# Transposed attention blocks written to DRAM in two copies and read by one transfer, and the split of v by a sign

## The chip, the cores and the metric

The kernel runs on one core of a Trainium2 chip. The metric is the time of one execution on the device in microseconds (us), the median of the runs shown. The engines of the core are TensorE (PE, with its weight loads PEld), VectorE (DVE), ScalarE (ACT), GpSimd (POOL) and SyncE (SP), which issues all DMAs of this kernel on one queue.

## What is computed

Attention within chunks of 64 tokens, then a layer with the elementwise maximum of three products. The reference, cut:

```python
# q, k, v: (batch 8, heads 8, seq 576, head_dim 64), chunk = 64, scale = 1/sqrt(64)
scores = scale * np.matmul(q_c, k_c.transpose(0, 1, 2, 4, 3))
scores = scores - np.max(scores, axis=-1, keepdims=True)
attn = np.exp(scores)
attn = attn / (np.sum(attn, axis=-1, keepdims=True) + 1e-09)
out = np.matmul(attn, v_c)
...
# x: (4608 tokens, 512), w1, w2, w3: (512, 768), w_out: (768, 512)
h = np.maximum(np.maximum(x @ w1, x @ w2), x @ w3)
return (h @ w_out).astype(np.float32)
```

All in float32.

## The kernel before

**Number format.** PE multiplies operands that are rounded to a narrower form (fp32r). To keep the accuracy, an operand is split into a high part (a rounding copy on ACT) and a low part (operand minus high part), and `three` adds three matmuls: high by low, low by high, high by high. One such trio of 128x512 is called a block here. Where both operands carry their parts, the products of the attention use another form: one operand is stacked, high part in partitions 0 to 63 and low part in 64 to 127, and the other holds high and low side by side in the free direction; a matmul then gives two sums that are added on the way out of PSUM (`products`: ACT copies one, VectorE adds the other).

**Tiles.** The tokens are 36 tiles of 128 (two chunks each, eight heads), in nine groups of four. The first eight tiles go through `plain_steps` at the start of the kernel, written in an order by hand (`FIRST`). The other 28 go through `attention`, whose steps are spread among the matmuls of the layer of earlier groups (`moe`; the last two groups are done together in `pair`). The tail after the last tile does no attention.

**One tile in `attention`.** r (q and k, two loads of 512 KB) is split into qs (stacked) and kk (side by side). Two products s, one for each chunk of the tile (steps s0 and s1), are summed into e by `sa0` and `sa1`. Then: maximum (`mx`, VectorE), subtraction (`sub`, POOL), exponential (`exp`, ACT), sum, guard and reciprocal (`sum`, VectorE), normalization (`nrm`, POOL), transpose of 32x32 blocks (`T`, VectorE) into et, high part (`ah`, ACT) and low part (`al`, VectorE) of et into the tile ah. The transposed blocks have to change partitions, so SP writes ah to a DRAM tile called there (`there`), waits, and reads it back as aa (`aa`), twice, into partitions 0 to 63 and 64 to 127, since v is stacked with its high part in the one half and its low part in the other. v (rv, 512 KB, each value in both halves) becomes vs: rounding copy of all 128 partitions on ACT (`vh`), and rv minus that copy in partitions 64 to 127 on POOL (`vl`, in `stack`, L311). Two products x of vs and aa (steps x0 and x1, in one bank of PSUM after another use of it) are summed into xs, or into the tile stage for the last two groups; where there is no stage, xs is split into xh (`xh`, ACT) and xl (`xl`, VectorE) for the layer. The tiles rv, kk, qs, r, ah and aa have one buffer each.

**What sets the order.** Inside `tc.manual_schedule` the instructions of each engine stand in the order in which the code emits them, and each engine works in that order. `due` collects a tile's steps with a time each: the table `AT` for the first four of these tiles, `MOVED` on top of it for the other 24. The main loop counts 0.6815 us for a block and 0.49 us for four products, and emits each step when its time has come. So the numbers of the tables only place a step between blocks; on the chip it starts when its semaphores allow. `TIMES` puts the tiles 18.0 us apart at first and 14.9 us from the fifth on. `FIRST_MIXED` places the first combinations of weights for `pair`.

Of the kernel before, what the change touches and what calls it, by code (L numbers as in the profile page):

```python
# [9 lines left out]
F32 = mybir.dt.float32  # L10
F32R = mybir.dt.float32r
# [3 lines left out]
AF = mybir.ActivationFunctionType  # L15
ALU = mybir.AluOpType
AX = mybir.AxisListType
# [3 lines left out]
P = 128  # L21
# [11 lines left out]
MOVED = {'r0': -18.9, 'r1': -14.6, 'rv': 7.3, 'qh': -8.4, 'ql': -7.2, 'kh0': -7.1, 'kl0': -6.2, 'kh1': -5.6, 'kl1': -1.4, 'sa0': 1.3, 's1': 3.3, 'sa1': 4.3, 'mx': 4.6, 'sub': 5.9, 'exp': 6.9, 'sum': 7.9, 'nrm': 9.1, 'T': 10.5, 'ah': 11.6, 'al': 11.7, 'there': 13.9, 'aa': 16.3, 'vh': 16.8, 'vl': 18.3, 'x0': 24.6, 'xa0': 25.6, 'x1': 28.3, 'xa1': 29.6, 'xh': 30.6, 'xl': 31.4}  # L33
EVERY = [18.3, 15.6]
OPERANDS = 5.4
FIRST_MIXED = 5.6
# [35 lines left out]
def chunk_attn_maxout_kernel(  # L72
# [12 lines left out]
    nc = tc.nc  # L85
# [21 lines left out]
    make_identity(nc, ident)  # L107

# [160 lines left out]
    def attention(t, x_of, col, every, stage=None, moved=()):  # L269
# [11 lines left out]
        def due(at, pe=0.0):  # L281
            return lambda fn: ops.append((at, pe, fn))
# [103 lines left out]
        @due(at_["al"])  # L386
        def _():
            nc.vector.tensor_tensor(out=st["ah"][:, :, 1], in0=st["et"], in1=st["ah"][:, :, 0].bitcast(F32), op=ALU.subtract)

        @due(at_["there"])  # L390
        def _():
            st["there"] = dram.tile([4, 64, 512], F32, name="there")
            nc.sync.dma_start(out=st["there"].rearrange("n (l k) f -> (n l) k f", k=2),
                              in_=st["ah"].bitcast(F32).rearrange("p k a n x -> p k (a n x)"))

        @due(at_["aa"])
        def _():
            st["aa"] = att.tile([P, 4, 2, 8, 32], F32R, name="aa", tag="aa", bufs=1)
            for rows in halves_of:
                nc.sync.dma_start(out=st["aa"][rows].bitcast(F32).rearrange("p n a g x -> p n (a g x)"),  # L400
                                  in_=st["there"].rearrange("n p f -> p n f"))

        stack(at_["vh"], at_["vl"], "vs", f"vs{t % 2}", lambda: st["rv"], nc.gpsimd)
# [17 lines left out]
        @due(at_["xl"])  # L421
        def _():
            xh, xl = x_of()
            nc.vector.tensor_tensor(out=xl[:, :, col:col + P], in0=st["xs"], in1=xh[:, :, col:col + P].bitcast(F32),
                                    op=ALU.subtract)
# [496 lines left out]
```

## Time and profile before

| | |
|---|---|
| median of 3 runs | 714.03 us (713.11 to 722.75) |
| profiled execution | 720.41 us, of which its span is 718.6 us |
| mean granted clock of PE | 0.983 |
| bytes moved by DMA | 125.93 MB, mean 175 GB/s |
| the queue of SP | busy 57.8% of 16 engines' span |

In the rows of the waits stand the engine and line that waited, what it waited for, the total in us, the number of waits and the longest. In the chain stand start, duration and what ran. In the groups of instructions stand line, engine, operation, output and inputs, shapes, count, busy time in us, mean duration in ns, and behind the second bar the idle time before them with what ended it; rows with three durations split by slashes give the least, the median and the greatest in ns. In the rows of DMA issues stand count, size of each and median us from issue to landing. In the rows of windows stand the window, its length, busy time and count of PE, PEld, DVE, ACT and POOL, the granted clock, the busy share of the DMA engines and GB/s. An arrow "x<-aa,vs" names output and inputs by the tiles' names. L289 is the matmul of the attention products, L169 to L171 the three of a block, L300 the sum on the way out of PSUM.

### The profile page before, as it was taken

The numbers are of one execution on the slowest core, as the hardware profiler recorded it, in microseconds if no ns is written. First come the engines' busy times: TensorE is split into PE (matmuls) and PEld (weight loads), VectorE is DVE, ScalarE is ACT, GpSimd is POOL, SyncE is SP. The second block draws the span as 40 slices with busy tenths as digits, with TensorE's granted clock in tenths as the row PEclk, the third lists the DMA queues.
The fourth block names the chain that finished last, engine by engine and source line by source line (L and its number), as shares of the span: only waits on it lengthen the run. The fifth ranks groups of instructions, "written<-read, shape, count | busy, mean of one in ns | idle before, by whom it ended". The sixth has DMA issues, their size and how long they took to land.

```text
span 718.6 us, 9620 instructions
## 1 busy us (share of the span) xinstructions
PE 691.3 (96%) x3336; PEld 574.5 (80%) x3336; DVE 516.7 (72%) x868; ACT 376.5 (52%) x695; POOL 249.9 (35%) x182
## 2 busy tenths in 40 slices
PE   8999999998899999999999998999989999999997
PEld 5998888887778777878877777878778888888876
DVE  6699984777668876898577876788657486768630
ACT  4476754554655566566656654566555352334221
POOL 1232201333334344222432332223323438666510
PEclk9599999999999999999999999999999999999999
DMA  8765554565787879667887767677784401011011
GB/s 344 304 226 180 205 176 138 173 207 172 224 258 215 220 209 277 177 202 213 236 232 194 214 175 236 195 212 193 194 257 123 131 30 59 29 31 26 5 55 63
DMA packets 44944, 125.93 MB, mean 175 GB/s; under 512 B 4192, under 2 KB 4192, under 8 KB 44896
## 3 DMA queue, kind: packets, MB, share of 16 engines
q1 hardware_dynamic: 44896, 125.32, 57.8%
q8 instruction: 26, 0.43, 0.3%
q14 instruction: 22, 0.18, 0.1%
HBM read 98.83 MB, written 26.48 MB: 174 GB/s over the span
## 4 chain that ended last, share of the span: by engine, by line
PE 29%; DMA 15%; DVE 13%; POOL 8%; ACT 4%; issue 3%; SPq 1%; POOLq 0%; ACTq 0%; DVEq 0%
DMA aa<-there 11%; PE pm L169 8%; PE pm L171 8%; PE pm L170 8%; DMA there<-ah 4%; PE x L289 3%; POOL c L537 2%; PE s L289 2%; POOL e L667 2%; DVE c L543 2%; POOL m L670 1%; DVE e L300 1%; POOL e L186 1%; POOL f L523 1%; ACT e L295 1%
## 5 line engine op out<-in xcount | busy, mean ns | idle before, releaser
L169 PE MATMUL pm<-xh,wl 128*128 128x512 f32 (+1 forms) x516 | 201.7, 391 | 0.0
L171 PE MATMUL pm<-xh,wh 128*128 128x512 f32 (+1 forms) x516 | 200.5, 389 | 0.0
L170 PE MATMUL pm<-xl,wh 128*128 128x512 f32 (+1 forms) x516 | 200.2, 388 | 0.0
L311 POOL TENSOR_TENSOR vs<-rv,vs 64x1024 fp32r<-64x1024 f32 x28 | 67.2, 2401 | 205.9 <-ACT vs L307 160.4
L171 PEld LDWEIGHTS pm<-xh,wh 128*128 128x128 f32 x516 | 98.0, 190 | 20.6
L169 PEld LDWEIGHTS pm<-xh,wl 128*128 128x128 f32 x516 | 98.3, 191 | 16.6
L170 PEld LDWEIGHTS pm<-xl,wh 128*128 128x128 f32 x516 | 98.1, 190 | 16.6
L300 DVE TENSOR_TENSOR e<-s,e 64x256 f32<-64x256 f32 x112 | 47.2, 422 | 47.6 <-ACT e L295 46.4
L458 DVE TENSOR_TENSOR m<-pm,m 128x512 f32<-128x512 f32 (+1 forms) x86 | 58.2, 677 | 11.9 <-PE pm L171 9.7
L169 PE MATMUL pm<-woh,h 128*128 128x512 f32 x168 | 65.6, 391 | 0.0
L170 PE MATMUL pm<-wol,h 128*128 128x512 f32 x168 | 65.6, 390 | 0.0
L171 PE MATMUL pm<-woh,h 128*128 128x512 f32 x168 | 65.5, 390 | 0.0
L186 POOL TENSOR_TENSOR e<-e,sm 128x512 f32<-128x512 f32 x30 | 37.6, 1253 | 73.4 <-DVE sm L183 58.4
L289 PEld LDWEIGHTS x<-aa,vs 128*128 128x128 f32 x224 | 32.4, 188 | 32.0 <-issue 17.5
L289 PE MATMUL x<-aa,vs 128*128 128x256 f32 x224 | 37.8, 291 | 20.0 <-DMA aa<-there 16.2
L295 ACT COPY e<-s 64x256 f32<-64x256 f32 x112 | 41.1, 367 | 28.5 <-PE s L289 27.5
L359 POOL TENSOR_TENSOR e<-e,mx 128x512 f32<-128x512 f32 x28 | 36.9, 1318 | 37.3 <-DVE mx L355 37.3
L464 ACT CAST h<-m 128x512 fp32r<-128x512 f32 (+1 forms) x43 | 26.2, 609 | 41.6 <-DVE m L458 41.4
L295 ACT COPY xs<-x 64x256 f32<-64x256 f32 x80 | 29.4, 368 | 33.2 <-PE x L289 32.5
L300 DVE TENSOR_TENSOR xs<-x,xs 64x256 f32<-64x256 f32 x80 | 33.4, 417 | 12.4 <-ACT xs L295 10.5
L337 DVE TENSOR_TENSOR kk<-r,kk 128x512 fp32r<-128x512 f32 x56 | 41.3, 739 | 1.0 <-ACT kk L333 0.8
L311 DVE TENSOR_TENSOR qs<-r,qs 64x1024 fp32r<-64x1024 f32 x28 | 37.5, 1340 | 6.1 <-ACT qs L307 5.4
(121 smaller groups left out, 1293.6 us busy)
## 6 DMA issues: line engine op xcount, KB each, us to landing
r<-in_qk SPq DMA_DIRECT2D x56, 512.0 KB, 4.6
aa<-there SPq DMA_DIRECT2D x56, 512.0 KB, 6.8
rv<-in_v SPq DMA_DIRECT2D x28, 512.0 KB, 5.5
there<-ah SPq DMA_DIRECT2D x28, 512.0 KB, 2.8
out_x<-ao SPq DMA_DIRECT2D x36, 256.0 KB, 2.1
buf<-in_qk SPq DMA_DIRECT2D x8, 768.0 KB, 7.2
buf<-in_w SPq DMA_DIRECT2D x10, 512.0 KB, 3.4
buf<-in_vb SPq DMA_DIRECT2D x8, 512.0 KB, 4.3
```

The lines of the kernel that those rows point to most:

```text
L169: nc.tensor.matmul(out=o, lhsT=al, rhs=bh, start=first, stop=False)
L170: nc.tensor.matmul(out=o, lhsT=ah, rhs=bl, start=False, stop=False)
L171: nc.tensor.matmul(out=o, lhsT=ah, rhs=bh, start=False, stop=last)
L186: eng.tensor_tensor(out=e, in0=e, in1=sm.unsqueeze(2).broadcast_to([P, 8, 64]), op=ALU.mult)
L289: nc.tensor.matmul(out=o[:, g].rearrange("p a h x -> p (a h x)"), lhsT=lhs(g), rhs=rhs(g), start=True, stop=True)
L295: nc.scalar.copy(out=out()[rows], in_=st[name][rows, :, 0, h, :])
L300: nc.vector.tensor_tensor(out=out()[rows], in0=st[name][rows, :, 1, h, :], in1=out()[rows], op=ALU.add)
L311: eng.tensor_tensor(out=st[name][64:], in0=src()[64:], in1=st[name][64:].bitcast(F32), op=ALU.subtract)
L337: nc.vector.tensor_tensor(out=st["kk"][:, c, :, 1, :], in0=st["r"][:, 1, c], in1=st["kk"][:, c, :, 0, :].bitcast(F32), op=ALU.subtract)
L359: nc.gpsimd.tensor_tensor(out=e_all(), in0=e_all(), in1=st["mx"].unsqueeze(2).broadcast_to([P, 8, 64]), op=ALU.subtract)
L458: nc.vector.tensor_tensor(out=banks[j][:, :n], in0=ps[j, w][:, :n], in1=banks[j][:, :n], op=ALU.max)
L464: nc.scalar.copy(out=hh[j][:, lo:hi], in_=banks[j][:, :hi - lo])
```

## The change

For each of the 28 tiles of `attention`:

- The write of ah goes out in two copies by one DMA: there is 1 MB instead of 512 KB, and each pair of its rows appears twice, next to itself.
- One DMA reads it into all 128 partitions; before, two read the same 512 KB into 64 partitions each. High and low parts of v therefore no longer lie in the two halves: partition 4l + 2h + k holds the high part for h = 0 and the low part for h = 1, and the host lays out v in that order.
- Since an instruction works on a range of partitions and the parts now alternate in pairs, vs is made in all partitions at once: ACT makes rv times a sign (+1 for high, -1 for low, from the new tile `sign_of`), rounded; VectorE then adds rv times 0 or 1 (`is_low`), over 128x1024 elements. `is_low` and `sign_of` are made by two operations on VectorE at the start.
- The subtractions `al` (28 times) and `xl` (20 times) go from VectorE to POOL, and `vl` from POOL to VectorE.
- Most numbers of `MOVED` change by 0.1 to 3.3 us and `FIRST_MIXED` by 0.2.

```diff
-MOVED = {... 'al': 11.7, 'there': 13.9, 'aa': 16.3, 'vh': 16.8, 'vl': 18.3, 'x0': 24.6, 'xa0': 25.6, 'x1': 28.3, ...}
+MOVED = {... 'al': 13.7, 'there': 13.9, 'aa': 17.5, 'vh': 17.4, 'vl': 18.6, 'x0': 25.1, 'xa0': 26.1, 'x1': 28.6, ...}
-FIRST_MIXED = 5.6
+FIRST_MIXED = 5.4
...
+    is_low, sign_of = (cpool.tile([P, 1], F32, name=n) for n in ("is_low", "sign_of"))
+    nc.vector.tensor_reduce(out=is_low, in_=ident.rearrange("p (l h k) -> p l h k", h=2, k=2)[:, :, 1], axis=AX.XY, op=ALU.add)
+    nc.vector.tensor_scalar(out=sign_of, in0=is_low, scalar1=-2.0, scalar2=1.0, op0=ALU.mult, op1=ALU.add)
...
         @due(at_["al"])
         def _():
-            nc.vector.tensor_tensor(out=st["ah"][:, :, 1], in0=st["et"], in1=st["ah"][:, :, 0].bitcast(F32), op=ALU.subtract)
+            nc.gpsimd.tensor_tensor(out=st["ah"][:, :, 1], in0=st["et"], in1=st["ah"][:, :, 0].bitcast(F32), op=ALU.subtract)
...
-            st["there"] = dram.tile([4, 64, 512], F32, name="there")
-            nc.sync.dma_start(out=st["there"].rearrange("n (l k) f -> (n l) k f", k=2),
-                              in_=st["ah"].bitcast(F32).rearrange("p k a n x -> p k (a n x)"))
+            st["there"] = dram.tile([4, P, 512], F32, name="there")
+            nc.sync.dma_start(out=st["there"].rearrange("n (l h k) f -> (n l) h (k f)", h=2, k=2),
+                              in_=st["ah"].bitcast(F32).rearrange("p k a n x -> p (k a n x)").unsqueeze(1)
+                              .broadcast_to([P, 2, 1024]))
...
-            for rows in halves_of:
-                nc.sync.dma_start(out=st["aa"][rows].bitcast(F32).rearrange("p n a g x -> p n (a g x)"),
-                                  in_=st["there"].rearrange("n p f -> p n f"))
-
-        stack(at_["vh"], at_["vl"], "vs", f"vs{t % 2}", lambda: st["rv"], nc.gpsimd)
+            nc.sync.dma_start(out=st["aa"].bitcast(F32).rearrange("p n a g x -> p n (a g x)"),
+                              in_=st["there"].rearrange("n p f -> p n f"))
...
+            nc.scalar.activation(out=st["vs"], in_=st["rv"], func=AF.Copy, scale=sign_of)
...
+            nc.vector.scalar_tensor_tensor(out=st["vs"], in0=st["rv"], scalar=is_low, in1=st["vs"].bitcast(F32),
+                                           op0=ALU.mult, op1=ALU.add)
...
-            nc.vector.tensor_tensor(out=xl[:, :, col:col + P], in0=st["xs"], in1=xh[:, :, col:col + P].bitcast(F32),
+            nc.gpsimd.tensor_tensor(out=xl[:, :, col:col + P], in0=st["xs"], in1=xh[:, :, col:col + P].bitcast(F32),
```

What the table makes of the order shows at three places, all in the steady part, at the seventeenth of the 28 tiles. On SP's queue, before, from the write of one tile to its second load of r:

```order
L393 DMA there<-ah 128x1024
L320 DMA r<-in_qk 128x1024
L400 DMA aa<-there 64x4x512 x2
L325 DMA rv<-in_v 128x1024
L320 DMA r<-in_qk 128x1024
```

And in the changed kernel:

```order
L396 DMA there<-ah 256x1x1024
L323 DMA r<-in_qk 128x1024
L403 DMA aa<-there 128x4x512
L328 DMA rv<-in_v 128x1024
L323 DMA r<-in_qk 128x1024
```

The sequence is the same; the write has twice the rows, and one read stands for two. Next, VectorE from the transpose of one tile (et) to the maximum of the next (mx), before:

```order
L379 STREAM_TRANSPOSE et<-e 128x512
L300 TENSOR_TENSOR xs<-x,xs 64x4x64 x2
L388 TENSOR_TENSOR ah<-et,ah 128x2x256
L337 TENSOR_TENSOR kk<-r,kk 128x4x128
L458 TENSOR_TENSOR m<-pm,m 128x512
L300 TENSOR_TENSOR xs<-x,xs 64x4x64 x2
L300 TENSOR_TENSOR e<-s,e 64x4x64 x2
L424 TENSOR_TENSOR xl<-xs,xh 128x4x128
L458 TENSOR_TENSOR m<-pm,m 128x512
L300 TENSOR_TENSOR e<-s,e 64x4x64 x2
L467 TENSOR_TENSOR h<-m,h 128x512
L355 TENSOR_REDUCE mx<-e 128x8
```

The same stretch in the changed kernel, where the names are the same and the lines have moved:

```order
L382 STREAM_TRANSPOSE et<-e 128x512
L303 TENSOR_TENSOR xs<-x,xs 64x4x64 x2
L340 TENSOR_TENSOR kk<-r,kk 128x4x128
L469 TENSOR_TENSOR m<-pm,m 128x512
L303 TENSOR_TENSOR xs<-x,xs 64x4x64 x2
L340 TENSOR_TENSOR kk<-r,kk 128x4x128
L303 TENSOR_TENSOR e<-s,e 64x4x64 x2
L469 TENSOR_TENSOR m<-pm,m 128x512
L413 SCALAR_TENSOR_TENSOR vs<-rv,is_low,vs 128x1024
L478 TENSOR_TENSOR h<-m,h 128x512
L303 TENSOR_TENSOR e<-s,e 64x4x64 x2
L358 TENSOR_REDUCE mx<-e 128x8
```

The low parts of ah and xl are gone, the second low part of kk has come into this stretch, and the low part of vs stands, with a low part of h, ahead of the sum of the second score product and the maximum. Last, POOL over one tile, before:

```order
L186 TENSOR_TENSOR e<-e,sm 128x512
L311 TENSOR_TENSOR vs<-rv,vs 64x1024
L359 TENSOR_TENSOR e<-e,mx 128x512
L186 TENSOR_TENSOR e<-e,sm 128x512
L311 TENSOR_TENSOR vs<-rv,vs 64x1024
```

And in the changed kernel:

```order
L189 TENSOR_TENSOR e<-e,sm 128x512
L391 TENSOR_TENSOR ah<-et,ah 128x2x256
L435 TENSOR_TENSOR xl<-xs,xh 128x4x128
L362 TENSOR_TENSOR e<-e,mx 128x512
L189 TENSOR_TENSOR e<-e,sm 128x512
```

Between the normalization of one tile and the subtraction of the next now stand the low part of ah and that of an earlier tile's xl, instead of the low part of vs.

On PE no instruction is added or removed. Counted in its order, 28 blocks stand between the second score product (s1) and the first product x (x0) of a tile before, and 29 in the changed kernel, for 24 of the 28 tiles (the first four keep 27 or 28); between x0 and x1 there are 5 blocks before and 4 in the changed kernel. x1 keeps its place.

9 lines of the change are left out of this document (7 added, 2 removed).

## The prediction

> **What bounds the kernel now.** I read the busy shares first, then what TensorE (PE) waits for, then the chain that ended last, then the transfers.
>
> ```profile
> span 718.6 us, 9620 instructions
> PE 691.3 (96%) x3336; PEld 574.5 (80%) x3336; DVE 516.7 (72%) x868; ACT 376.5 (52%) x695; POOL 249.9 (35%) x182
> ```
>
> PE is idle in only 718.6 - 691.3 = 27.3 us. The change adds and removes no matmul, so whatever it can win is in those microseconds, and in the speed of PE around them. The waits of PE name nearly all of them:
>
> ```profile
> PE x L289 <- DMA aa<-there: 16.2, 14, 2.5
> PE x L289 <- issue: 2.7, 2, 1.4
> PE s L289 <- DVE e L300: 1.3, 3, 0.7
> ```
>
> The first row is the product x of the transposed probabilities aa with v: 14 times it waited for the read of aa from DRAM. The two waits called "issue" stand at the same product (at 317 and 509 us), with SP, DVE and ACT long done, so I count them to aa too: 18.9 us in 16 of 28 tiles. The chain shows what is late, here from one tile's maximum to its x:
>
> ```profile
> 343.51 0.70 DVE mx L355
> 344.34 2.03 POOL e L359
> ...
> 351.33 0.70 DVE ah L388
> 352.05 2.98 DMA there<-ah
> 355.71 8.77 DMA aa<-there
> 364.62 0.73 PE x L289 x4
> ```
>
> Of 21 us, 12 lie in the write of the block and its read back. Nothing stands between the end of ah on VectorE (352.03) and the write (352.05): a microsecond less or more in this chain moves the x of that tile by as much, until the wait is zero.
>
> The long waits cost more than their length.
>
> ```profile
> 167.63 0.72 PE L289 MATMUL x<-aa,vs 128*128 128x256 f32 x4 [2.47 <-DMA aa<-there]
> 206.80 0.72 PE L289 MATMUL x<-aa,vs 128*128 128x256 f32 x4 [1.74 <-DMA aa<-there]
> 364.62 0.71 PE L289 MATMUL x<-aa,vs 128*128 128x256 f32 x4 [1.64 <-DMA aa<-there]
> 444.69 0.72 PE L289 MATMUL x<-aa,vs 128*128 128x256 f32 x4 [2.29 <-DMA aa<-there]
> 522.43 0.39 PE L170 MATMUL pm<-xl,wh 128*128 128x512 f32 x1
> 523.11 0.39 PE L170 MATMUL pm<-xl,wh 128*128 128x512 f32 x1
> 526.58 0.71 PE L289 MATMUL x<-aa,vs 128*128 128x256 f32 x4 [2.18 <-DMA aa<-there]
> 528.88 0.63 PE L169 MATMUL pm<-xh,wl 128*128 128x512 f32 x1
> 529.31 0.63 PE L170 MATMUL pm<-xl,wh 128*128 128x512 f32 x1
> 430.00:460.00 30.00, 27.06 (x125) 22.13 (x124) 19.05 (x35) 15.99 (x31) 8.20 (x5) 0.94 0.82 237
> ```
>
> Before the wait of 2.18 us three matmuls take 523.11 - 522.43 = 0.68 us (one block); after it one takes 529.31 - 528.88 = 0.43 instead of 0.23. Around the wait of 2.29 the granted clock (the third number from the end of the last row, a stretch of 30 us) is 0.94: (1 - 0.94) x 30 = 1.8 us lost. I price both so. The wait of 2.47 cost no clock. So about 3.5 us of the profiled execution go with two long waits. The Trainium skill ("TensorE: Matmul & The Clock Gate", "What's actually happening") says that the clock halves after a whole idle window of about 3.4 us that runs freely. The trace disagrees on the length, since a wait of 2.2 us was enough; if the slow clock came from something else, the sum below would be 3.5 us higher.
>
> **The transfers.** Each tile writes ah (512 KB) once and reads it twice, into partitions 0 to 63 and 64 to 127.
>
> ```profile
> aa<-there SPq DMA_DIRECT2D x56, 512.0 KB, 6.8
> there<-ah SPq DMA_DIRECT2D x28, 512.0 KB, 2.8
> buf<-in_w SPq DMA_DIRECT2D x10, 512.0 KB, 3.4
> f<-whole SPq DMA_DIRECT2D x8, 256.0 KB, 2.6
> 481.40:482.40 1.00, 1.00 (x8) 0.91 (x7) 0.91 (x3) 0.73 (x2) 0.00 (x0) 1.00 0.85 348
> 486.80:489.60 2.80, 2.80 (x14) 2.31 (x13) 2.07 (x4) 1.66 (x3) 2.63 (x2) 1.00 1.06 225
> 477.20:478.20 1.00, 0.58 (x5) 0.61 (x6) 0.79 (x2) 0.00 (x0) 0.64 (x1) 1.00 0.97 365
> ```
>
> The last number of the first four rows is the median time to landing; the last two of the others are the busy share of the DMA engines and GB/s. From 481.4 us a write of ah runs alone: 348 / 0.85 = 409 GB/s of busy engines. From 477.2 a load into all 128 partitions runs: 365 / 0.97 = 376. From 486.8 only the two reads of aa run: 225 / 1.06 = 212, about half, with the engines fully busy. Each of these reads goes to 64 partitions; every other transfer goes to 128.
>
> **The change, part by part**, for one tile, along the chain:
>
> - One read for two. By the two landings of 128-partition loads, 256 KB more cost 0.8 us, so 1 MB lands 3.4 + 2 x 0.8 = 5.0 us after its issue. f<-whole also reads rows of 2 KB from DRAM, as aa does. Now the later of the two halves lands 6.8 us (median) to 8.8 (chain) after its own issue, which is 0.6 after the first: about 8.2 from the first. I take -3.2, with -4.4 as the good end; the bad end, if the rate stays 212, is -0.4.
> - The block is written twice: 0.52 MB more at 409 GB/s, +1.3 us.
> - The low part of ah on GpSimd (POOL):
>
> ```profile
> L388 DVE TENSOR_TENSOR ah<-et,ah 128x512 fp32r<-128x512 f32 x28 | 19.3, 691 | 2.1 <-ACT ah L384 1.4
> L424 DVE TENSOR_TENSOR xl<-xs,xh 128x512 fp32r<-128x512 f32 x20 | 13.8, 692 | 0.5
> L186 POOL TENSOR_TENSOR e<-e,sm 128x512 f32<-128x512 f32 x30 | 37.6, 1253 | 73.4 <-DVE sm L183 58.4
> L359 POOL TENSOR_TENSOR e<-e,mx x28: 1042/1048/2019, 110.8 to 554.7; 128x512 f32<-128x512 f32 x28
> L311 POOL TENSOR_TENSOR vs<-rv,vs 64x1024 fp32r<-64x1024 f32 x28 | 67.2, 2401 | 205.9 <-ACT vs L307 160.4
> L311 DVE TENSOR_TENSOR qs<-r,qs x28: 1222/1223/2108, 93.9 to 540.7; 64x1024 fp32r<-64x1024 f32 x28
> L153 DVE SCALAR_TENSOR_TENSOR ao<-buf,ao 128x512 uint32<-128x512 uint32 x16 | 10.9, 687 | 0.1
> L307 ACT CAST vs<-rv 128x1024 fp32r<-128x1024 f32 x28 | 29.4, 1049 | 0.2
> ```
>
>   A two-input operation of this shape takes 1.25 us on POOL (L186) against 0.69 on VectorE: +0.55, between +0.35 (L359's least, 1.04) and +1.3 (its greatest, 2.02).
> - The low part of v leaves POOL (2.40 us) for VectorE as one operation of 128x1024. No row has it; L153 does half as many columns in 0.69, L311 (least, median and greatest in its row) as many in 1.22, so 1.3 us. It takes the place of the low part of x (0.69), ahead of the sum of the second score product and the maximum: +0.6 in the chain. The ends are 0 (VectorE idles there anyway: 46.4 us in all, below) and +1.4 (2.1, the longest L311, less 0.69).
> - The low part of x on POOL: after the low part of ah, ahead of the next tile's subtraction of the maximum. POOL loses 2.40 and gains 2 x 1.25 a tile, and is busy 35%: nothing. Should x's high part be late, the subtraction behind it would wait up to 1.25.
> - The high part of v with a scale for each partition: same elements as L307, 1.05 us, nothing. The two new operations at the start stand where VectorE idles for its first load (the last row below): nothing.
> - The order of PE: from tile 5 on, x comes 29 blocks after the second score product, not 28: 0.68 us more before it is late. The second x now follows the first after 4 blocks (2.7 us) instead of 5, and both use one bank. The first's evacuation (0.75 on ACT, 0.86 on VectorE, then it is free) leaves some 0.3 us. The score products already stand 4 blocks apart and waited 3 times, 1.3 us in all; I take 1.5 us.
>
> ```profile
> DVE e L300 <- ACT e L295: 46.4, 42, 3.5
> SPq L393 <- DVE ah L388: 97.9, 25, 7.6
> 5.00 0.43 DVE L149 TENSOR_SCALAR ao<-ao 128x512 uint32<-128x512 uint32 x1 [3.61 <-ACT ao L141]
> ```
>
> In the second row SP waits for ah itself in 25 of 28 writes, so no other DMA on SP's queue delays the write; behind it on that queue stand only loads that are wanted a tile later.
>
> **The sum.** Per tile: -3.2 + 1.3 + 0.55 + 0.6 - 0.68 = -1.4 us against the moment when x is wanted; for the first four tiles, without the extra block, -0.75. Of the 16 waits, those of 2.47, 2.29, 2.18, 1.74 and 1.64 leave 1.7 + 0.9 + 0.8 + 0.3 + 0.2 = 3.9, all others go: -15.0 us. The clock comes back: -3.5. The second x costs +1.5. The profiled execution took 720.4 (the span and 1.8 around it): 720.4 - 15.0 - 3.5 + 1.5 = 703.4. The median, 714.0, lies 6.4 lower. I read that as an execution without the slow clock (3.5) and with 2.9 us less of waits, which no row here shows; then 714.0 - (18.9 - 2.9 - 3.9 - 1.5) = 703.4 as well. I forecast **703**.
>
> **Rivals.**
>
> *The read stays slow.* If 212 GB/s is not due to the 64 partitions but to what is read (rows of 2 KB, four far apart in DRAM), one transfer takes as long as the two. Then per tile: -0.4 + 1.3 + 0.55 + 0.6 - 0.68 = +1.4. The 16 waiting tiles give 22 us, the other 12 perhaps 0.5 each, and some six waits pass 2 us and halve the clock at 1.8: 714 + 22 + 6 + 11 + 1.5 = about 754; with VectorE's term at zero and the write partly beside it, +0.5 a tile, about 730. It decides from a rate below some 300 GB/s on. Against it: only the reads to 64 partitions run at 212, and f<-whole with the same rows lands in 2.6. Chance 0.09. The Trainium skill speaks on both sides: "SBUF — State Buffer", "Door 1: The DMA port swizzle", has 64 partitions reach 8 of the 16 ports, 218 against 436 GB/s (the trace: 212 against 376 to 409); by its 436 the one read would move its data in 2.4 us. "DMA: Bandwidth & Descriptors", "Latency and other measured facts", found row pitches of large powers of two slow (207 GB/s at 512 KiB); the blocks here lie 128 KB apart, and 256 KB in the changed kernel.
>
> *The gain is given back on VectorE and POOL.* If POOL's and VectorE's two-input operations hold each other up, as L359's 2.02 against 1.04 and L311's 2.1 against 1.22 suggest, the terms are +1.3 and +1.4: per tile -3.2 + 1.3 + 1.3 + 1.4 - 0.68 = +0.1, no gain, 714; half of that, or a second x that waits 0.3 us in 24 tiles (7 us), gives 709. Chance 0.29. The Trainium skill has such a lock ("SBUF — State Buffer", "Who interferes with whom"): a VectorE operation with two inputs in SBUF and a GpSimd one that reads it exclude each other whole. L359's 2.02 agrees; its median of 1.05 says that they seldom meet.
>
> *The read gains its full 4.4.* All 16 waits go and the evacuation never bites: 714.0 - 18.9 + 2.9 = 698 or less. Chance 0.22, everything below 700.
>
> **How the numbers follow.** The forecast, 700 to 706, has 0.36, the second rival, 706 to 716, 0.29; between 716 and 728 I leave 0.04. The range 695 to 716 holds these two and most of the good case. 2% of 714 is 14.3 us, about what a measurement tells from no change, so faster is below 699.7: the good case and, since the edge lies close to the forecast, 0.04 of that: 0.26. Slower is the first rival, 0.09; the rest is 0.65.
>
> **What would show it.** The read of aa should land about 5 us after its issue and the write after about 4.1; a window with the read alone should show over 350 GB/s. PE's wait for aa should fall from 16.2 to some 4 us, with a granted clock of 1.00 in the steady part, and waits of x for xs or stage on VectorE should stay under 3 us. ah on POOL should take near 1.25, vs on VectorE near 1.3. A landing of 8 us, or a maximum that comes over a microsecond later after the second score product, proves me wrong.

## The result, and the profile after

The changed kernel is slightly slower: 717.59 us, median of 20 runs (714.12 to 729.12), against 714.29 us (710.64 to 726.98) for the kernel before on the same chip; the ratio is 1.0055, with a 95% interval of 1.0033 to 1.0076. I had forecast 703, range 695 to 716.

The head of the page of the changed kernel, span and busy time of the engines:

```profile
span 715.3 us, 9546 instructions
PE 685.4 (96%) x3336; PEld 563.4 (79%) x3336; DVE 534.1 (75%) x850; ACT 380.1 (53%) x695; POOL 246.0 (34%) x202
```

This execution took 717.08 us, near its median; that of before took 720.41, above its own. The two spans can't be set against each other as they stand. Executions of one kernel differ in this way: of the six of e9 below, three have a mean granted clock of 0.985 to 0.988 and took 708.1 to 708.9 us, the other three one of 0.997 to 1.000 and took 701.6 to 703.8. Windows of the start of the kernel before:

```profile
0.00:20.00 20.00, 17.92 (x94) 12.54 (x95) 13.73 (x26) 9.23 (x14) 3.33 (x9) 0.90 0.91 352
20.00:40.00 20.00, 20.00 (x124) 20.00 (x124) 12.98 (x24) 10.83 (x21) 6.38 (x6) 0.67 0.80 306
```

and the second of them in the changed kernel:

```profile
20.00:40.00 20.00, 20.00 (x177) 20.00 (x176) 19.16 (x40) 16.80 (x33) 8.87 (x7) 1.00 0.97 371
```

The profiled execution of before ran part of its first 40 us at a low clock (0.90 and 0.67), and that of after did not. The second score product of its first tile in `attention` starts at 107.64 us, that of after at 100.44. The stretch from there to the second score product of the last tile is called the steady part below. It takes 443.9 us before and 447.8 after: 4 us longer, in agreement with the medians. So the loss is in the steady part. What PE waited for there, in the waits of the changed kernel:

```profile
PE x L292 <- DMA aa<-there: 10.1, 12, 2.6
PE s L292 <- DVE e L303: 3.7, 4, 1.2
PE s L292 <- ACT vs L409: 2.2, 3, 1.0
PE s L292 <- DVE kk L340: 1.7, 6, 0.4
```

The waits for aa fell from 18.9 to 10.1 us, not to 4, and the waits at the score products s grew from 1.3 us to these three rows, 7.6 in all. The idle time of the weight loads (PEld) shows both places whole. Groups of instructions, before:

```profile
L289 PEld LDWEIGHTS x<-aa,vs 128*128 128x128 f32 x224 | 32.4, 188 | 32.0 <-issue 17.5 <-POOL e L186 4.7 <-POOL e L359 4.6
L289 PEld LDWEIGHTS s<-kk,qs 128*128 128x128 f32 x224 | 34.0, 188 | 7.1 <-ACT xh L419 1.4 <-ACT e L295 1.1 <-DVE kk L337 0.3
```

and after:

```profile
L292 PEld LDWEIGHTS x<-aa,vs 128*128 128x128 f32 x224 | 32.3, 188 | 26.5 <-issue 6.0 <-DVE m L469 4.8 <-DVE sm L186 4.7
L292 PEld LDWEIGHTS s<-kk,qs 128*128 128x128 f32 x224 | 32.5, 188 | 19.8 <-ACT vs L409 4.3 <-DVE kk L340 4.0 <-ACT xh L430 3.0
```

The number behind the second bar is the idle time: at x it falls by 5.5 us, at s it rises by 12.7. The matmuls themselves idle less, but in the same sense: from 20.0 down to 14.4 us at x, from 1.3 up to 8.5 at s. So s is the place of the loss. The transfers after, with the median landing as the last number:

```profile
r<-in_qk SPq DMA_DIRECT2D x56, 512.0 KB, 4.9
there<-ah SPq DMA_DIRECT2D x28, 1024.0 KB, 4.4
aa<-there SPq DMA_DIRECT2D x28, 1024.0 KB, 7.3
```

The write is near the forecast 4.1. The read takes 7.3 instead of 5.0. Yet its rate is as forecast: the last read runs alone, and in this window 401 / 1.04 = 386 GB/s of busy engines are moved (225 / 1.06 = 212 before):

```profile
567.00:568.40 1.40, 1.40 (x8) 1.17 (x7) 0.69 (x1) 0.59 (x2) 0.20 (x1) 1.00 1.04 401
```

The timeline of one tile's write and read shows what went wrong (start, duration, engine, line, output and inputs; kk of the next tile, r of the one behind it):

```profile
331.44 1.28 POOL L391 TENSOR_TENSOR ah<-et,ah 128x512 fp32r<-128x512 f32 x1 [1.48 <-ACT ah L387]
331.60 1.68 DVE L340 TENSOR_TENSOR kk<-r,kk 128x512 fp32r<-128x512 f32 x1
332.75 0.52 SPq L396 DMA_DIRECT2D there<-ah  x1
333.67 0.64 PE L292 MATMUL s<-kk,qs 128*128 128x256 f32 x4
334.40 0.75 ACT L298 COPY e<-s 64x256 f32<-64x256 f32 x2 [0.48 <-PE s L292]
334.82 0.69 DVE L340 TENSOR_TENSOR kk<-r,kk 128x512 fp32r<-128x512 f32 x1
335.54 0.33 SPq L323 DMA_DIRECT2D r<-in_qk  x1
336.15 0.85 DVE L303 TENSOR_TENSOR e<-s,e 64x256 f32<-64x256 f32 x2
337.12 0.53 PEld L292 LDWEIGHTS s<-kk,qs 128*128 128x128 f32 x4 [0.50 <-ACT h L475]
337.14 0.38 SPq L403 DMA_DIRECT2D aa<-there  x1
337.15 0.71 PE L292 MATMUL s<-kk,qs 128*128 128x256 f32 x4
```

Both low parts of kk (L340) stand late on VectorE. The second ends at 335.51, and at 335.54 SP issues the load of r that had waited for this buffer: 2.8 us behind the write and 1.6 us ahead of the read, so that its 512 KB lie on the queue in front of aa. In the kernel before a load of r lay there too, nearer to the write (1.3 us behind it by the median, 2.8 after); the same three DMAs of the tile that the prediction showed:

```profile
352.05 0.33 SPq L393 DMA_DIRECT2D there<-ah  x1
354.31 0.39 SPq L320 DMA_DIRECT2D r<-in_qk  x1
355.08 1.24 SPq L400 DMA_DIRECT2D aa<-there  x2
```

In the 22 tiles from the fifth on that have such a load, it was issued ahead of the read by 2.0 us before and 1.6 after, and landed 2.4 and 3.1 us behind the read's issue (medians). In tiles 2 and 27, where no load lies ahead, the two reads landed in 7.5 and 7.6 us before and the one in 5.7 and 5.3 after; over tiles 5 to 28 the means are 8.2 and 7.3. So the 8.2 us that I counted for the two reads held a share of r, some 0.7, and the 5.0 that I counted for the one read, from loads with nothing in front, did not; after, r costs 1.6 to 2.0.

And VectorE, kept busy by the two low parts and what had queued up behind them, starts the sum of the first score product at 336.15, 1.0 us after ScalarE's copy of it (334.40 + 0.75); the second score product, which needs the bank, goes on 0.15 us after that sum has ended. The profile puts the wait of 0.50 us down to another engine's h, which had ended 0.2 us earlier. Waits of SP's queue, before and after, a fence each:

```profile
SPq L320 <- DVE kk L337: 10.8, 19, 1.0
```

```profile
SPq L323 <- DVE kk L340: 48.1, 20, 3.8
```

The loads of r are now held back by kk for 48.1 us in all, not 10.8.

### The profile page after: what moved, and what is told of

The parts are those of the page before. It is cut to its first block, busy times and chain, and to the rows that moved or that the text cites. A ratio compares the mean times of both kernels' runs of the same rounds, so it can differ in the third digit from the quotient of the medians.

```text
span 715.3 us, 9546 instructions
## 1 busy us (share of the span) xinstructions
PE 685.4 (96%) x3336; PEld 563.4 (79%) x3336; DVE 534.1 (75%) x850; ACT 380.1 (53%) x695; POOL 246.0 (34%) x202
## 4 chain that ended last, share of the span: by engine, by line
PE 39%; DMA 21%; DVE 19%; POOL 10%; ACT 6%; issue 5%; SPq 0%; POOLq 0%; DVEq 0%; ACTq 0%
DMA aa<-there 13%; PE pm L172 11%; PE pm L174 11%; PE pm L173 11%; DMA there<-ah 5%; PE x L292 3%; POOL c L548 2%; PE s L292 2%; PE x L255 2%; DVE m L469 2%; DVE kk L340 2%; POOL e L678 2%; POOL e L189 2%; DVE c L554 2%; DVE e L303 1%
## 5 line engine op out<-in xcount | busy, mean ns | idle before, releaser
L362 POOL TENSOR_TENSOR e<-e,mx 128x512 f32<-128x512 f32 x28 | 42.2, 1507 | 150.8 <-DVE mx L358 150.8
L340 DVE TENSOR_TENSOR kk<-r,kk 128x512 fp32r<-128x512 f32 x56 | 57.6, 1030 | 1.4
L189 POOL TENSOR_TENSOR e<-e,sm 128x512 f32<-128x512 f32 x30 | 33.4, 1112 | 65.0 <-DVE sm L186 62.1
L292 PEld LDWEIGHTS x<-aa,vs 128*128 128x128 f32 x224 | 32.3, 188 | 26.5 <-issue 6.0
L391 POOL TENSOR_TENSOR ah<-et,ah 128x512 fp32r<-128x512 f32 x28 | 36.8, 1316 | 43.7 <-ACT ah L387 43.7
L292 PE MATMUL x<-aa,vs 128*128 128x256 f32 x224 | 38.0, 292 | 14.4 <-DMA aa<-there 10.1
L292 PEld LDWEIGHTS s<-kk,qs 128*128 128x128 f32 x224 | 32.5, 188 | 19.8 <-ACT vs L409 4.3
L435 POOL TENSOR_TENSOR xl<-xs,xh 128x512 fp32r<-128x512 f32 x20 | 27.8, 1389 | 56.8 <-ACT xh L430 56.8
```

The source lines that it names most:

```text
L189: eng.tensor_tensor(out=e, in0=e, in1=sm.unsqueeze(2).broadcast_to([P, 8, 64]), op=ALU.mult)
L292: nc.tensor.matmul(out=o[:, g].rearrange("p a h x -> p (a h x)"), lhsT=lhs(g), rhs=rhs(g), start=True, stop=True)
L340: nc.vector.tensor_tensor(out=st["kk"][:, c, :, 1, :], in0=st["r"][:, 1, c], in1=st["kk"][:, c, :, 0, :].bitcast(F32), op=ALU.subtract)
L362: nc.gpsimd.tensor_tensor(out=e_all(), in0=e_all(), in1=st["mx"].unsqueeze(2).broadcast_to([P, 8, 64]), op=ALU.subtract)
L391: nc.gpsimd.tensor_tensor(out=st["ah"][:, :, 1], in0=st["et"], in1=st["ah"][:, :, 0].bitcast(F32), op=ALU.subtract)
L435: nc.gpsimd.tensor_tensor(out=xl[:, :, col:col + P], in0=st["xs"], in1=xh[:, :, col:col + P].bitcast(F32), op=ALU.subtract)
```

## The experiments

All ratios are against the kernel before on the same chip, with 95% intervals; the changed kernel has 1.0055 on this scale. "Idle at x" and "idle at s" are the idle times of the weight loads, as above (before 32.0 and 7.1, after 26.5 and 19.8).

### Code and table apart

```diff
 # e1: the changed code with MOVED and FIRST_MIXED of before
 # e2: the code of before with MOVED and FIRST_MIXED of the change
```

> The changed kernel with the table of step times (and FIRST_MIXED) of before, all else as changed: x0 is back to 28 blocks after s1, x1 5 blocks after x0, and the low parts of kk and the load r1 stand early again. Theory A (the table: r is held back by the late low part of kk and lies in the queue ahead of aa, and the score products wait for late kk): aa lands 5 to 6 us after its issue instead of 7.3, PE's weight loads idle at s 8 us instead of 19.8, and the time is 706 to 711, below both kernels. Theory B (the code: low part of ah on POOL and of v on VectorE hold each other and the evacuations up): the idle time at s stays near 20 us, x0 loses its extra block, and the time is 717 to 725.

> The kernel before with the table of step times (and FIRST_MIXED) of the changed one: two reads of 64 partitions, all engines as before, x0 29 blocks after s1, kk and r1 late. Theory A: r now lies ahead of the slow reads too, so they come 1 to 1.5 us later against 0.68 us more room, and s waits as in the changed kernel (idle 15 to 20 us): 722 to 730. Theory B: the table alone is harmless or helps by its block: idle at s stays near 7 us, waits of x shrink, 706 to 713.

Measured: e1 719.79 us, 1.0066 (1.0028 to 1.0105), idle at x 36.1, at s 5.4. e2 740.23 us, 1.031 (1.0251 to 1.0369), idle at x 47.7, at s 13.1. Of the two numbers forecast for e1, 706 to 711 is missed, and 717 to 725 is met without the idle time at s that was to bring it. e2 lies above both of its ranges. The new table by itself is bad (3.1% in the old code), and it brings idle time at s in either code; the new code by itself loses too, at x, where x0 stands only 28 blocks after s1 as before. In the table of the change the new code is worth 2.5 points.

### The low parts of kk

```diff
 # e3, in the changed kernel's MOVED
-'r1': -13.3, 'kl0': -3.2, 'kl1': 0.1
+'r1': -14.6, 'kl0': -6.2, 'kl1': -1.4
 # e12: only 'kl1': -1.4
 # e14: only 'kl0': -6.2 and 'r1': -14.6
 # e11: the code of before with e3's table
```

> The changed kernel with three numbers of its table set back to those of before: kl0 -6.2, kl1 -1.4 (low parts of kk) and r1 -14.6 (load of the second half of r). Theory A: SP's waits for kk fall from 48 us to some 11, r is issued over 2 us before aa, aa lands 5 to 6 us after its issue, idle at x falls from 26.5 to under 15 us and at s from 19.8 to under 10: 703 to 709. Theory B: r comes early, but the low part of kk still takes 1.03 us on VectorE and the idle time at s stays near 20: 713 to 718.

e3 took 707.13 us, ratio 0.9885 (0.9825 to 0.9944): faster than both kernels. On PE, ScalarE and GpSimd nothing moves against the changed kernel, and on SP's queue one pair of DMAs near the end. Waits, groups and transfers of e3:

```profile
PE x L292 <- DMA aa<-there: 12.4, 11, 3.2
PE x L292 <- DVE xs L303: 6.1, 8, 1.4
```

```profile
L292 PEld LDWEIGHTS s<-kk,qs 128*128 128x128 f32 x224 | 34.0, 188 | 6.4 <-ACT vs L409 0.9 <-ACT xh L430 0.8 <-issue 0.5
L292 PEld LDWEIGHTS x<-aa,vs 128*128 128x128 f32 x224 | 32.4, 191 | 31.5 <-issue 12.1 <-ACT ah L387 7.7 <-DVE kk L340 3.9
```

```profile
there<-ah SPq DMA_DIRECT2D x28, 1024.0 KB, 5.2
aa<-there SPq DMA_DIRECT2D x28, 1024.0 KB, 5.5
```

The idle time at s goes back from 19.8 to 6.4; at x, where under 15 was expected, it even rises by 5.0; and the time, as expected, falls by 1.7 points (12 us; 7.3 by the steady parts of the two profiled executions). So it is the place of kk's low parts on VectorE that costs, and it costs at the score products. The read now lands in 5.5, because r is issued 0.6 us behind the write and lands 1.2 us after the read's issue (medians), not 3.1; the write, which now shares the queue with it, takes 5.2 instead of 4.4.

> The changed kernel with the place of one step alone changed: kk's second low part stands where it stood before the change (-1.4, not 0.1), so that it is not between the two score products' sums. Theory L1 (that low part, in the way of the first score product's sum, is the cost at the score products): the idle time of weight loads at s falls from 19.8 us to below 10, 706 to 710. Theory L2 (it is the first low part, 3 us later than before, that holds the next r back or holds the first score product): idle at s stays above 15 us, 713 to 718.

> The changed kernel with kk's first low part where it stood before the change (-6.2, not -3.2; the load behind it at -14.6, as before), and the second left late. Theory L2 (the first low part, late, holds the next load of r and with it the score products): idle time of weight loads at s falls from 19.8 us below 12, aa lands in under 6 us, 707 to 711. Theory L3 (only both together help, since one of the two always stands ahead of the first score product's sum): idle at s stays above 15, 712 to 717.

e12: 712.51 us, 0.9955 (0.9921 to 0.9988). e14: 715.06 us, 0.9989 (0.9956 to 1.0022). SP's waits and the group at s, of e12 and of e14:

```profile
SPq L323 <- DVE kk L340: 15.1, 16, 1.3
```

```profile
L292 PEld LDWEIGHTS s<-kk,qs 128*128 128x128 f32 x224 | 32.2, 188 | 19.6 <-DVE kk L340 6.5 <-ACT xh L430 6.2 <-ACT e L298 1.5
```

```profile
SPq L323 <- DVE kk L340: 39.7, 21, 3.2
```

```profile
L292 PEld LDWEIGHTS s<-kk,qs 128*128 128x128 f32 x224 | 33.4, 188 | 10.6 <-ACT vs L409 2.5 <-issue 2.4 <-ACT h L475 1.5
```

The two do different harm. The second low part, late, holds back the load of r: SP waits 15.1 us for kk with it early (e12), 39.7 with the first early (e14), 48.1 with neither. The first, late, makes most of the idle time at s: 19.6 with the second early, 10.6 with the first, 6.4 with both. e14 met its expectation at s, not in time, nor at aa, which still lands in 6.9 us. e12 has the idle time of its second theory, and a time between its two ranges. Each alone wins 0.7 to 1.0 points, both together 1.7.

> The kernel before the change with the table in which kk's low parts are early (and the changed kernel's places for all other steps). Theory K1 (the early low parts of kk are the whole gain, whoever transfers the blocks): 705 to 712, under the kernel before. Theory K2 (the early kk only takes back what the changed table lost, and the gain under the kernel before comes from the one read): 718 to 732, with PE's waits for aa at 18 us or more.

e11: 725.75 us, 1.0116 (1.0052 to 1.018), waits for aa 20.1 in 17 tiles, as the second theory had it. The early kk alone isn't the gain: in this table, with the other steps where the change put them, the old code is 1.2% slower than with its own, and the new code is 2.3 points better than the old. Code and table need each other.

### What the read and its place on the queue are worth

```diff
 # e4: the changed kernel; aa read as two transfers of 64 partitions, each from its own copy
-            nc.sync.dma_start(out=st["aa"]..., in_=st["there"]...)
+            for rows in halves_of:
+                nc.sync.dma_start(out=st["aa"][rows]..., in_=st["there"][:, rows]...)
 # e5: e3 with the load of r behind the read of aa
-'r1': -14.6
+'r1': -11.0
```

> The changed kernel with its one read of aa cut into two transfers, partitions 0 to 63 and 64 to 127, each from its own copy in DRAM. If the 64 partitions set the rate (212 GB/s in the kernel before), a window with these reads alone shows about 210 GB/s of busy engines again, aa lands 2 to 3 us later, and the time is 735 to 765. If the rate of before came from both transfers reading the same addresses, the rate stays near 370 to 400 GB/s, only the second issue (0.6 us) is added, and the time is 717 to 724.

> As the kernel with kk and r early (kl0 -6.2, kl1 -1.4; 707 us), but r1 -11.0, so the load of r's second half is issued behind the read of aa instead of between the write and that read. Theory C (r's 512 KB between them eat most of what the read won: write and read land in 5.2 + 5.5 us there): the write lands in 4.1 to 4.4, the read in 5.0 to 5.5, x waits less, 699 to 704. Rival D (the queue is not the matter; r is now late for kk): idle at s rises over 10 us from 6.4, 707 to 715.

e4: 759.01 us, 1.0601 (1.0553 to 1.0649), waits for aa 42.1 us in 23 tiles. A window of e4 in which, by the order of the queue, only the reads run:

```profile
345.50:347.00 1.50, 1.50 (x8) 1.27 (x7) 1.50 (x1) 1.50 (x3) 0.42 (x1) 1.00 1.00 228
```

228 GB/s against the 386 of the whole read, though each half now has its own copy: the 64 partitions set the rate. From the first issue to the last landing the two reads take 9.0 us and the one of the changed kernel 7.3 (means of tiles 5 to 28), with r issued 1.6 us ahead of both. e4 has the changed kernel's table and code and only the read in halves, so the one read over 128 partitions is worth 5.5 points there. e5: 725.26 us, 1.0124 (1.0068 to 1.0179). With r out of the way the write lands in 4.3 us and the read in 5.4, 9.7 in all (forecast 9.1), and the waits for aa are 3.5 us in 5 tiles. But the time lies above both ranges: r comes too late for the next tile's kk, and VectorE waits 30.9 us for kk's high part:

```profile
L340 DVE TENSOR_TENSOR kk<-r,kk 128x512 fp32r<-128x512 f32 x56 | 55.1, 986 | 31.6 <-ACT kk L336 30.9
```

Behind it the second x waits for the evacuation of the first (17.5 us in 14 tiles, and 6.2 where it goes to stage). The load can't be moved out of the way for nothing.

### The second copy

```diff
 # e6: e3 with ah written once, by two DMAs, and read by one that gives every row to two partitions
+            st["there"] = dram.tile([32, 2, 4, 512], F32, name="there")
+            for k in range(2):
+                nc.sync.dma_start(out=st["there"][:, k].rearrange("l n f -> n l f"), in_=st["ah"][:, k]...)
 # e9: e3 with ah written once as before (512 KB), read by four DMAs (the low parts of v in the odd partitions, as in e6)
-            nc.sync.dma_start(out=st["aa"]..., in_=st["there"]...)
+            for n in range(4):
+                nc.sync.dma_start(out=st["aa"][:, n].bitcast(F32).rearrange("p a g x -> p (a g x)"),
+                                  in_=st["there"][n].unsqueeze(1).broadcast_to([64, 2, 512]))
```

> As the kernel with kk and r early (707 us), but the block is written once (two transfers of 256 KB, rows of 2 KB) and read by one transfer of 128 partitions that reads each row of DRAM twice; v and the sign are laid out to match (low parts in odd partitions). Theory C: the second half megabyte of the write cost 1.3 us a tile; write lands in about 3.3 us, read in 5 to 5.5, wait of x for aa falls from 12.4 to under 5 us: 698 to 703. Rival E (the rate of the read depends on the two copies, as reading the same rows twice is slow): the read lands in 7 us or more, 708 to 720.

> The table with kk's low parts early; the block is written once (512 KB) and read by four transfers of 256 KB into all 128 partitions, each row of DRAM going to two neighbouring partitions. Theory T1 (the second copy in the write costs its full time on the path to x): the write lands in 2.8 to 3.3 us instead of 5.2, PE's waits for aa fall from 12.4 us below 5, the waits for x0's evacuation stay, and the time is 699 to 704. Theory T2 (three more issues of a DMA on SP, and smaller packets of the queue behind r, give it back): the last read starts 1 to 1.5 us later, the waits for aa stay at 10 us or more, and the time is 705 to 712.

e6: 799.74 us, ratio 1.1172. It tells nothing of the second copy, since its write is slow. Two lines of its SP queue for one tile, between which a load of r is issued:

```profile
352.68 1.10 SPq L397 DMA_DIRECT2D there<-ah  x2
362.35 0.56 SPq L403 DMA_DIRECT2D aa<-there  x1
```

Two writes of 256 KB need 9.7 us until the read may go out, against 3.1 on the mean for one of 512 KB in e9. Their outermost dimension is the four blocks. A window of e6 in which the writes are still under way:

```profile
360.00:362.30 2.30, 2.30 (x11) 1.90 (x11) 2.19 (x5) 1.01 (x2) 0.70 (x1) 1.00 0.23 86
```

The DMA engines are busy to 0.23 and move 86 GB/s, as if 4 of 16 worked. The Trainium skill ("DMA: Bandwidth & Descriptors", "Rules for kernel authors") says that an outermost dimension below 16 confines a DMA to at most as many engines; the row agrees.

e9: 705.93 us, 0.9839 (0.978 to 0.9897). The waits for aa are gone from the list. The longest and the transfers:

```profile
PE x L292 <- DVE xs L303: 9.0, 10, 3.2
```

```profile
there<-ah SPq DMA_DIRECT2D x28, 512.0 KB, 2.9
aa<-there SPq DMA_DIRECT2D x112, 256.0 KB, 4.2
```

Without the second copy the read goes out 3.1 us after the write and not 5.2 (means of tiles 5 to 28 of e9 and e3), and the reads land in time although there are four to issue. So the second copy takes 2.1 us of the chain, not 1.3, when r shares the queue. The four reads give some of it back: from the first issue to the last landing they take 6.8 us, the one read of e3 5.8. The waits fell as the first theory of e9 had it, the median came as the second had it, and the ratio is hardly under e3's, with intervals that overlap. But the profiled execution of e9 also had the low clock at its start, where e3's had 1.00:

```profile
20.00:40.00 20.00, 20.00 (x119) 20.00 (x120) 12.87 (x25) 10.37 (x20) 5.98 (x5) 0.64 0.86 322
```

The steady parts, which this doesn't touch, are 432.0 us in e9 and 440.5 in e3: 8.5 us less. The waits for aa that went are 12.4 us, and the second x waits 2.9 longer for the evacuation of the first, so in these two executions most of the freed time came back. The ratio shows only some 3 us of it.

### The blocks between the products

```diff
 # in e3's table (x0 25.1, xa0 26.1, x1 28.6, xa1 29.5):
 # e7:  'x0': 25.8, 'xa0': 26.8, 'x1': 29.3, 'xa1': 30.2, 'xh': 32.1, 'xl': 35.4    (30 blocks after s1)
 # e10: 'x1': 29.3, 'xa1': 30.2                                                    (x1 five blocks after x0)
 # e15: 'x0': 24.4, 'xa0': 25.4                                                    (x0 28 blocks after s1, x1 five after x0)
 # e16: 'x0': 24.4                                                                 (the same, the evacuation not moved)
 # e13 and e17: as e15 and e16, in e9
```

> As the kernel with kk and r early (707 us), but x0 and x1 and all that follows them in a tile 0.7 us later: 30 blocks after s1 instead of 29. If the waits of x are late DMA alone, each shrinks by 0.68 us: 12.4 us for aa become 5 to 7, time 701 to 704. If the evacuations of x1 then meet those of the next score product (x1 now stands right ahead of it), idle at s rises over 10 us and the time stays at 706 to 712.

> The table with kk's low parts early; the second product x comes five blocks after the first, as before the change, not four. If the evacuation of the first x in the way of the second (waits for xs on VectorE, 6.1 us) is a cost of the changed order: these waits go, 701 to 704. If the second x, now right ahead of the next tile's first score product, only hands the wait on (the score product waits, or the evacuations of x1 and s0 meet on ScalarE and VectorE): 706 to 715, with PE's waits at s above 4 us.

> The version with kk's low parts early and one read, and the first product x one block earlier (28 blocks after the second score product, five ahead of the second x). Theory P1 (the block between the two products is worth more than the block ahead of the first): waits for x0's evacuation fall from 6.1 us below 2, those for aa rise from 12.4 us by less than 6, and the time is 702 to 707. Theory P2 (the block ahead of the first x was a gain, as forecast: 0.68 us in each tile that waits): waits for aa rise to 20 us or more, 710 to 716.

> The kernel with one write and four reads, and the first product x one block earlier (28 blocks after the second score product, five ahead of the second x). Theory X1 (the waits for x0's evacuation, 9.0 us there, come from the nearness of the two products): they fall below 3 us, waits for aa rise from 0 to 1 to 4 us since the slack there is about a block, and the time is 698 to 703. Theory X2 (VectorE is late with the evacuation whatever the distance, or the block was needed for aa): waits of x for xs or aa stay at 7 us or more in sum, 704 to 710.

> The version with kk's low parts early and one read; the first product x alone stands a block earlier (28 blocks after the second score product, five ahead of the second x), its evacuation stays behind the next tile's transpose on VectorE. Theory P1 (the nearness of the two products costs most of the 6.1 us of waits for xs): those waits fall below 2 us, waits for aa rise from 12.4 us by less than 8, the transpose again ends about 1.0 us after the normalization, and the time is 704 to 711. Theory P2 (the block ahead of the first x is worth its 0.68 us in each tile): waits for aa rise to 22 us or more, 712 to 720.

> The kernel with one write and four reads; the first product x alone stands a block earlier, its evacuation stays behind the next tile's transpose. Theory X1 (aa has about a block to spare there, so the waits for xs, 9.0 us, go and nothing replaces them): waits of x for xs and aa below 4 us together, 697 to 703. Theory X2 (nothing to spare): waits for aa of 6 us or more, 704 to 709.

| run | us | ratio | waits for aa | waits for xs |
|---|---|---|---|---|
| e3 | 707.13 | 0.9885 (0.9825 to 0.9944) | 12.4 | 6.1 |
| e7 | 716.38 | 1.0007 (0.997 to 1.0043) | 4.3 | 12.3 |
| e10 | 715.63 | 0.9982 (0.9946 to 1.0018) | 14.3 | 2.9 |
| e15 | 729.42 | 1.0191 (1.015 to 1.0233) | 26.0 | none |
| e16 | 721.17 | 1.0088 (1.0047 to 1.0129) | 18.5 | 1.2 |
| e9 | 705.93 | 0.9839 (0.978 to 0.9897) | none | 9.0 |
| e13 | 709.59 | 0.99 (0.9861 to 0.9939) | 4.4 | 1.5 |
| e17 | 701.33 | 0.9834 (0.978 to 0.9887) | 2.0 | 5.8 |

e13 came out in its second range and e17 in its first; e7, e10, e15 and e16 came out above all of theirs. e15 and e13 did more than was meant: the evacuation of x0, put earlier with it, came ahead of the next tile's transpose on VectorE. ScalarE's wait for that transpose, in e15 and in e3:

```profile
ACT ah L387 <- DVE et L382: 26.5, 18, 2.3
```

```profile
ACT ah L387 <- DVE et L382: 12.2, 12, 1.8
```

e16 leaves the evacuation where it was. Taking the extra block ahead of x0 away then costs 2.0 points (8.0 us by the profiled spans). The waits are those of the first theory, the cost that of the second: the waits for xs fall to 1.2 us, those for aa rise by 6.1, and the mean granted clock of the profiled execution falls from 0.998 to 0.992, which is some 4 of the 8 us. With the block kept and x1 moved (e10) waits pass to the score products, whose idle time is 13.4. A block more for both (e7) takes the waits for aa down to 4.3 and brings 12.3 for xs. So the nearness of the two products goes with 5 to 6 us of waits in e3, and every other place that I tried costs more. With aa in time (e9, e17) the block can stand either way; the ratios are the same within their intervals. But there the distance is only part of it: with five blocks (e17) 5.8 of the 9.0 us of waits for xs are left, more than the first theory of e17 had for xs and aa together. What makes them is not shown. e9 and e17 beat the two kernels, by 1.6 to 1.7% against before.

### The low part of ah on VectorE again

```diff
-            nc.gpsimd.tensor_tensor(out=st["ah"][:, :, 1], ...)
+            nc.vector.tensor_tensor(out=st["ah"][:, :, 1], ...)
```

> The changed kernel with its own table, only the low part of ah back on VectorE. Theory B (POOL's and VectorE's two-input operations hold each other up): the low part of kk falls from 1.03 us to under 0.8, idle at s from 19.8 to under 12, 706 to 712. Theory A (kk's place in the order makes s wait, whatever its length): idle at s stays at 15 us or more, the chain is 0.45 us shorter, 713 to 718.

e8 (the changed kernel with this alone): 724.66 us, 1.0111 (1.0059 to 1.0163). The groups of kk in the changed kernel and in e8, mean ns behind the comma:

```profile
L340 DVE TENSOR_TENSOR kk<-r,kk 128x512 fp32r<-128x512 f32 x56 | 57.6, 1030 | 1.4
```

```profile
L340 DVE TENSOR_TENSOR kk<-r,kk 128x512 fp32r<-128x512 f32 x56 | 39.1, 700 | 1.3
```

kk's low parts are stretched by 0.33 us each when GpSimd splits ah beside them, in the timeline above one takes 1.68 us. The idle time at s falls from 19.8 to 13.6, between the two theories, so this stretching is probably a part of what kk costs there. Its place is the larger one, since in e3 kk's low parts are as long (1050 ns on the mean) and the idle time is 6.4. All the same e8 is no faster and lies above both ranges (its interval overlaps that of the changed kernel; the steady part is 2.8 us longer): the waits for aa rise from 10.1 to 19.6 us. On VectorE the low part of ah takes 0.68 us but ends 2.0 us after the high one (means of tiles 5 to 28), on GpSimd 1.4, because it has to wait its turn on VectorE.

## Why the prediction was wrong

- **What bounds the kernel: right.** The room was in the waits for aa and the clock; e9 takes all waits for aa away and is 1.6% faster.
- **One read for two, -3.2 us: the first step that failed.** The mechanism was right (386 GB/s, and 228 where e4 halves it), the size was not: from the issue of the read to the start of x the mean of tiles 5 to 28 went from 8.71 to 7.60 us, -1.1. The 5.0 us is near what the read takes with nothing in front (5.4 in e5); I set it against 8.2 us that held a load of r. With r in the same place the one read is worth 1.8 us (e4 against the changed kernel), with nothing ahead some 2 (tiles 2 and 27). I wrote that "no other DMA on SP's queue delays the write; behind it on that queue stand only loads that are wanted a tile later". A load that is wanted later still takes its share of the queue, and the order that I had shown has it between the write and the read. Write and read together took 9.7 us at best (e5), 10.7 with r right behind the write (e3) and 11.7 in the changed kernel (sums of the medians), against 9.1 in my sum.
- **The low parts of kk: no term at all.** I had shown that "the second low part of kk has come into this stretch", and gave it no price. It is the largest one: idle at s +12.7 us, and e3 wins 1.7 points by taking both low parts back. A term of 7 to 12 us would have taken most or all of the 11 us of gain that I forecast.
- **The write twice, +1.3: too small.** By the medians of landing +1.6 (2.8 to 4.4), and 2.1 between e9 and e3, where r lies right behind the write.
- **al on GpSimd, +0.55: right.** Its end came 1.39 us after that of the high part instead of 0.98, so +0.4. The second rival, that VectorE and GpSimd hold each other up, was right in another place: kk's low parts pay, +0.33 us each. The Trainium skill ("SBUF — State Buffer", "Who interferes with whom") has a VectorE operation with two inputs in SBUF and a GpSimd one that reads SBUF exclude each other; the 1.68 us of kk, which ends 0.56 us after the GpSimd operation beside it, agrees.
- **vl on VectorE, +0.6: too much.** Its length was right (1289 ns against 1.3 us), but the maximum ends 2.82 us after the second score product instead of 2.69: +0.1, near the good end that I gave.
- **The extra block ahead of x0, -0.68 in each tile: right, as far as e16 tells.** Over 16 waiting tiles that is 10.9 us; e16 against e3 has 8.0 by the spans, half of it the clock, and 14 by the ratios. The waits for aa themselves rise by 6.1 us, 0.5 in each of the 12 tiles that wait.
- **The second x after four blocks, +1.5: too small once aa comes in time,** 6 to 9 us in e3 and e9, though five blocks (e17) take only 3 of the 9 away. In the changed kernel itself no such wait stands in the list; x0 or s waited first.
- **The clock, -3.5 and the median: half right.** I let the clock of the long waits come back whole. From 100 to 550 us the mean granted clock is 0.99 before and 1.00 after, but the changed kernel still has one wait of 2.6 us for aa, ending at 279.77 us, and around it the clock falls as before:

```profile
270.00:300.00 30.00, 27.39 (x125) 22.39 (x125) 21.67 (x35) 15.92 (x30) 8.50 (x7) 0.94 0.64 219
```

  That is (1 - 0.94) x 30 = 1.8 us, so about half of the 3.5 came back. And that the profiled execution lay 6.4 us over the median I put down to this and to "2.9 us less of waits, which no row here shows". The rows of its first 40 us show it: (1 - 0.90) x 20 + (1 - 0.67) x 20 = 8.6 us by the granted clock.

## What to carry to other kernels

A landing time that is read from a busy queue may not be set against one from a free queue: list what lies ahead of the transfer in both, and what frees its buffer. Give every instruction that a table moves a term of its own, by what is queued behind it and who waits for that, however idle its engine is on the mean. And when code and order change together, run the four combinations: here the new code won 2.5 points in the new order and lost 0.7% in the old one.

## What the runs showed of the hardware that I had not expected

- A write whose outermost dimension is 4 kept the DMA engines busy to 0.23 only, and two of 256 KB took 9.7 us where one of 512 KB in another order lands in 2.9 (e6, e9).
- The profiled executions of before and of e9 ran at a granted clock of 0.67 and 0.64 from 20 to 40 us with PE fully busy, those of all other kernels here at 1.00. What decides it stays open.
- The length of a wait alone does not tell whether the clock falls. Around waits of 2.3 us (before, shown in the prediction) and 2.6 us (after, the row above) a stretch of 30 us has a granted clock of 0.94. Around one of 2.5 us (before, ending at 167.63 us) it is 1.00 from 155 to 185 us, and around one of 3.0 us in e3, ending at 360.03 us, it is 1.00 too:

```profile
345.00:375.00 30.00, 27.00 (x132) 22.52 (x131) 22.14 (x35) 16.20 (x30) 8.10 (x6) 1.00 0.76 260
```
